# Global keys folded into unused score rows, and q and k of two batches transposed by DMA

## The chip, the cores and the metric

The kernel runs on one core of a Trainium2 chip. The metric is the device time of one execution in microseconds (us), lower is better.

Words used below: PE is the TensorE (PEld its weight loads), DVE the VectorE, ACT the ScalarE, POOL the GpSimd, SP the SyncE, which here only issues DMAs. "L362" is line 362 of that kernel's source; the numbers shift between kernels, so the tile names are the better way to find a group. A DMA transfer is *issued* by an engine and *lands* when the last of its data has arrived. The rows marked PEclk, and the word "clock", give the clock that PE was granted, as a share of full speed.

## The reference, cut to what matters

```python
# B=4, H=8, S=768, D=64, n_global=8, n_local=96
scores = q @ k.T / sqrt(D)
keep   = is_global(key < 8) | is_local(0 <= query - key < 96)
dist   = 96 where global and not local, else |query - key|
a      = softmax(scores - slope[head] * dist, only where keep)
x      = (a @ v) as [B, S, H*D]                    # per batch 768 x 512
theta  = x @ w_theta
y      = w_tok_r @ (x*cos(theta)) + w_tok_i @ (x*sin(theta))
u      = x + y
out    = u + relu(u @ w_ch)
```

A query sees at most 96 keys behind it and the first 8 keys. With tiles of 128 tokens, a tile of 128 keys meets only its own tile of queries and the first 95 queries of the next one.

## The kernel before

The work is a pipeline over batches. While the PE does the second half of batch b (theta, then "mixing" with w_tok, then "chan" with w_ch), it is given the attention of batch b+1 in between. I call the stretch from the first theta product of one batch to the first theta product of the next a *stage*, and name it after the batch whose attention is done in it: the "stage for batch 2" holds the mixing of batch 1 and the attention of batch 2. Three stages follow a start of some 30 us, and the end of batch 3 comes last.

q and k must have their head dimension on the partitions. Before, one load of 768 KB brings each of q and k of a batch, DVE puts a pair of heads in the order that a transpose wants (`qkn`), PE transposes 12 blocks of 128x128, and DVE and ACT copy the result from PSUM:

```python
def prep(b, p, w=0):                        # one pair of heads
    qkn = att.tile([T, NT, 2, 2, D], BF, name="qkn", bufs=3)
    with behind("dve"):
        for i_ in range(2):
            (...)(out=qkn[:, :, i_]..., in_=qk[:, i_, 2 * p:2 * p + 2])
    for i_, dst in ((0, qT), (1, kT)):
        ps = ps_small([T, NT, T], BF)
        with behind("pe"):
            for t_ in range(NT):
                nc.tensor.transpose(ps[:, t_, :], qkn[:, t_, i_]..., ident)
        (vector.tensor_copy for q, scalar.copy for k)(out=dst as (n t), in_=ps)
```

The global keys have scores, exponentials and a value product of their own:

```python
def globals_(b):                            # per batch: 2 bursts of 8 products
    for hh in range(2):
        for p in range(NP):
            nc.tensor.matmul(pg[GS*p:GS*(p+1), c0:c1], lhsT=kT[R, 0:GS], rhs=qT[R, c0:c1])
        nc.scalar.activation(e_, pg[:, 0:S], AF.Exp, bias=gbias...)
        ...
def scores(b, p, c):                        # two tiles of keys, two heads
    ... nc.tensor.matmul(pb[:, hh, j*W:j*W+n], lhsT=kT[R, tile], rhs=qT[R, tile and 96 more])
def values(b, p, hh):                       # per query tile: own, previous, global
    mms = [(e own, vn[it])] + ([(e previous, vn[it-1])] if it else []) + [(eg, vg)]
```

The order in which a stage starts, and the DMA transposes that were there already:

```python
order = rest[:-1] + pre[:2] + th[:2] + pre[2:] + th[2:3] + rest[-1:] + th[3:]
...
nc.sync.dma_start_transpose(out=xT..., in_=x_sb...)   # xtrans, 6 blocks, feeds theta
nc.sync.dma_start_transpose(out=uT, in_=u)            # utrans, 4 blocks, feeds chan
```

q, k and v are loaded by POOL's queue two batches ahead, as soon as their buffers come free. Everything on SP is a DMA issue, done in order: xT, uT, and the output writes.

The softmax here doesn't subtract the row's maximum and nothing guards it: scores larger than these inputs give would overflow.

Of the kernel before, what the change touches and what calls it, by code (L numbers as in the profile page):

```python
# [16 lines left out]
def kernel(  # L17
# [15 lines left out]
    T = 128  # L33
# [26 lines left out]

    loads = {}

    def alloc_loads(b):
        qk = ld.tile([T, 2, H, NT, D], BF, name="qk", bufs=1)
        vn = ld.tile([T, H, NT, D + 1], BF, name="vn")
        nc.vector.memset(vn[:, :, :, D:D + 1], 1.0)
        loads[b] = (qk, vn)

    def load_qk(b, h0, n, which=(0, 1)):
        qk = loads[b][0]  # L70
        for i_ in which:
            nc.gpsimd.dma_start(
                out=qk[:, i_, h0:h0 + n].rearrange("p h t d -> p h (t d)"),
                in_=(q, k)[i_][b, h0:h0 + n].rearrange("h (p t) d -> p h (t d)", p=T))
# [8 lines left out]
    for p in range(NP):  # L83
        load_qk(0, 2 * p, 2)
    load_v(0, 0, 4)
    load_v(0, 4, 4)
# [3 lines left out]
    ones = const.tile([T, W], FP)  # L90
    nc.vector.memset(ones, 1.0)
    ramp = const.tile([T, W], FP)
# [10 lines left out]
    dist = const.tile([T, W], FP)  # L103
    nc.vector.tensor_scalar(dist, ramp, pidx, None, op0=ALU.subtract)
    far = const.tile([T, W], FP)
    nc.vector.tensor_scalar(far, dist, 0.0, None, op0=ALU.is_lt)
    nc.vector.scalar_tensor_tensor(far, in0=dist, scalar=float(NL), in1=far, op0=ALU.is_ge, op1=ALU.add)
    nc.vector.scalar_tensor_tensor(dist, in0=far, scalar=1e6, in1=dist, op0=ALU.mult, op1=ALU.max)
    etab = const.tile([T, H, W], BF)

    def bias_table(p):
        for h in (2 * p, 2 * p + 1):
            nc.scalar.activation(etab[:, h, :], dist, AF.Exp, scale=-slopes[h])


    NE = 4
    e_bufs = [const.tile([T, 2, NT, 2 * T], BF, name=f"e_{i_}") for i_ in range(NE)]
    e_cnt = [0]
    gbias = const.tile([T, 2], FP)
    gmask = const.tile([T, T], BF)  # L120
    shift = const.tile([T, NP, T], BF)
    halfpi = const.tile([T, 1], FP)
    junk = const.tile([T, 1], FP)

    def constants():

        for e_t in e_bufs:
            nc.vector.memset(e_t[:, :, :, W:2 * T], 0.0)


        grel = const.tile([T, T], FP, name="grel")
        nc.vector.tensor_scalar(grel, ramp[:, 0:T], kmod[:, 0:1], None, op0=ALU.subtract)
        for hh in range(2):
            for p in range(NP):
                nc.vector.memset(gbias[GS * p:GS * (p + 1), hh:hh + 1], -float(NL) * slopes[2 * p + hh])

        gneg = const.tile([T, 1], FP, name="gneg")
        nc.vector.tensor_scalar(gneg, grel[:, 0:1], -float(NG), -30000.0, op0=ALU.is_le, op1=ALU.mult)
        nc.vector.tensor_scalar(gbias, gbias, gneg, None, op0=ALU.add)

        gfar = const.tile([T, T], FP, name="gfar")
        nc.vector.tensor_scalar(gfar, grel, float(NL), None, op0=ALU.is_ge)
        nc.vector.scalar_tensor_tensor(gmask, in0=grel, scalar=0.0, in1=gfar, op0=ALU.is_lt, op1=ALU.add)

        nc.vector.memset(shift, 0.0)
        for p in range(NP):
            nc.vector.tensor_copy(out=shift[0:NG, p, GS * p:GS * p + NG], in_=ident[0:NG, 0:NG])
        nc.vector.memset(halfpi, HALF_PI)
# [33 lines left out]
    egs = {}  # L182
# [6 lines left out]

    def prep(b, p, w=0):  # L190
        qk = loads[b][0]
        if (b, 0) not in qkT:
            x_sb[b] = moe.tile([T, NP, NT, T], BF, name="x_sb", bufs=2)
            xT_sb[b] = moe.tile([T, NC, S], BF, name="xT", bufs=1)

        qkn = att.tile([T, NT, 2, 2, D], BF, name="qkn", bufs=3)
# [4 lines left out]
        qT = att.tile([T, S], BF, name="qT", bufs=6)  # L201
        kT = att.tile([T, S], BF, name="kT", bufs=6)
        for i_, dst in ((0, qT), (1, kT)):
            ps = ps_small([T, NT, T], BF)
            with behind("pe"):
                for t_ in range(NT):
                    nc.tensor.transpose(ps[:, t_, :], qkn[:, t_, i_].rearrange("p h d -> p (h d)"), ident)  # L207

            dst = dst.rearrange("p (n t) -> p n t", t=NT)
            src = ps.rearrange("p t n -> p n t")  # L210
            if i_ == 0:
                nc.vector.tensor_copy(out=dst, in_=src)  # L212
            else:
                nc.scalar.copy(out=dst, in_=src)  # L214
            if w:
                warm(w)
        qkT[(b, p)] = (qT, kT)

    def globals_(b):
        eg = []  # L220
        for hh in range(2):
            R = slice(D * hh, D * (hh + 1))
            pg = ps_big().rearrange("p a b -> p (a b)")
            for p in range(NP):
                qT, kT = qkT[(b, p)]
                for c0, c1 in ((0, 512), (512, S)):
                    nc.tensor.matmul(pg[GS * p:GS * (p + 1), c0:c1], lhsT=kT[R, 0:GS],
                                     rhs=qT[R, c0:c1], start=True, stop=True)
            e_ = att.tile([T, S], BF, name=f"eg_{hh}", bufs=2)
            nc.scalar.activation(e_, pg[:, 0:S], AF.Exp, scale=scale, bias=gbias[:, hh:hh + 1])  # L230
            nc.vector.tensor_mul(e_[:, 0:T], e_[:, 0:T], gmask)
            eg.append(e_)
        egs[b] = eg
# [3 lines left out]
    def scores(b, p, c):  # L237
        qT, kT = qkT[(b, p)]
        if c == 0:
            ebuf[(b, p)] = e_bufs[e_cnt[0] % NE]  # L240
            e_cnt[0] += 1
        e_t = ebuf[(b, p)]
        pb = ps_big()
        for j in range(2):
            jt = 2 * c + j
            n = min(W, S - jt * T)
            for hh in range(2):
                R = slice(D * hh, D * (hh + 1))
                nc.tensor.matmul(pb[:, hh, j * W:j * W + n], lhsT=kT[R, jt * T:(jt + 1) * T],  # L249
                                 rhs=qT[R, jt * T:jt * T + n], start=True, stop=True)  # L250
        jt = 2 * c
        if jt + 2 < NT:
            nc.scalar.activation(  # L253
                e_t[:, :, jt:jt + 2, 0:W],
                pb[:, :, 0:2 * W].rearrange("p a (j w) -> p a j w", j=2), AF.Exp, scale=scale)
            nc.vector.tensor_mul(
                e_t[:, :, jt:jt + 2, 0:W], e_t[:, :, jt:jt + 2, 0:W],
                etab[:, 2 * p:2 * p + 2, None, :].to_broadcast([T, 2, 2, W]))
        else:
            nc.scalar.activation(e_t[:, :, jt, 0:W], pb[:, :, 0:W], AF.Exp, scale=scale)  # L260
            last = nc.scalar.activation(e_t[:, :, jt + 1, 0:T], pb[:, :, W:W + T], AF.Exp, scale=scale).ins
            if p == NP - 1:

                with tc.issue_after(last):
                    nc.scalar.activation(junk, halfpi, AF.Sin)
            nc.vector.tensor_mul(e_t[:, :, jt, 0:W], e_t[:, :, jt, 0:W], etab[:, 2 * p:2 * p + 2, :])
            nc.vector.tensor_mul(e_t[:, :, jt + 1, 0:T], e_t[:, :, jt + 1, 0:T],
                                 etab[:, 2 * p:2 * p + 2, 0:T])

    vgs, pos = {}, {}  # L270

    def vglob(b, p):
        vn = loads[b][1]
        pv = ps_small([T, 2, D + 1], FP)
        nc.tensor.matmul(pv, lhsT=shift[:, p, :], rhs=vn[:, 2 * p:2 * p + 2, 0, :],
                         start=True, stop=True)
        vg = att.tile([T, 2, D + 1], BF, name="vg", bufs=4)
        nc.scalar.copy(out=vg, in_=pv)
        vgs[(b, p)] = vg

    def values(b, p, hh):
        vn = loads[b][1]
        e_t = ebuf[(b, p)]
        vg = vgs[(b, p)]
# [6 lines left out]
        for it in range(NT):  # L291
            mms = [(e_t[:, hh, it, 0:T], vn[:, 2 * p + hh, it, :])]
            if it:
                mms.append((e_t[:, hh, it - 1, T:2 * T], vn[:, 2 * p + hh, it - 1, :]))
            mms.append((egs[b][hh][:, it * T:(it + 1) * T], vg[:, hh, :]))
# [94 lines left out]
    def attention_steps(b):  # L390
# [5 lines left out]
        add(1500, globals_, b)  # L396
        for p in range(NP):
            add(150, vglob, b, p)
            if p + 1 < NP:
                add(900, scores, b, p + 1, 0)  # L400
            add(1100, values, b, p, 0)
            if p + 1 < NP:
                add(900, scores, b, p + 1, 1)
            add(1100, values, b, p, 1)
# [25 lines left out]
    with tc.manual_schedule(engines={mybir.EngineType.PE}):  # L430
        warm(8)
        prep(0, 0, 4)
        bias_table(0)
        for p in range(1, NP):
            prep(0, p, 2 if p == 1 else 0)
            bias_table(p)
            if p == 1:
                constants()
            for c in range(NT // 2):
                scores(0, p - 1, c)  # L440
                warm(1)
        globals_(0)
        for p in range(NP):
            vglob(0, p)
        scores(0, NP - 1, 0)
        for p in range(NP):
            values(0, p, 0)
            values(0, p, 1)
            if p < 2:
                scores(0, NP - 1, p + 1)  # L450
            if p:
                xtrans(0, p - 1, nc.scalar.copy)
# [73 lines left out]
```

## Time and profile before

| | before |
|---|---|
| median (lowest to highest) | 193.61 us (193.41 to 193.78) |
| span of the profiled execution | 190.0 us |
| first theta product of batch 0, 1, 2, 3 | 30.5, 77.4, 117.0, 157.2 us |
| stage for batch 1, 2, 3 | 46.9, 39.6, 40.2 us |

The head of the profile page of before: busy time per engine, then the busy tenths of PE and the granted PE clock in 40 slices.

```profile
span 190.0 us, 3965 instructions
PE 174.4 (92%) x1616; PEld 89.8 (47%) x1641; DVE 131.3 (69%) x305; ACT 108.0 (57%) x162; POOL 27.0 (14%) x31
...
PE   7868698999999999999999999999999999999981
PEclk9999999999999999999999999999999999999999
```

PE is at nine tenths from slice 8 on, and its clock is full throughout. The chain of work that ended last, by engine and by line, on the page of before:

```profile
PE 65%; ACT 15%; DVE 8%; DMA 6%; issue 3%; POOL 1%; ACTq 0%; SPq 0%; POOLq 0%
PE ps L352 27%; PE ps L377 10%; PE pb L333 9%; PE pb L298 7%; PE pb L249 5%; DMA uT<-u 3%; PE ps L207 3%; DMA qk<-in_k_dram 3%; ACT cs L337 2%; ACT kT L214 2%; ACT e_108 L253 2%; PE ps L170 2%; DVE qT L212 1%; DVE qkn L199 1%; DVE zri L341 1%
```

Most of the chain is PE work. The busy time by stretch (31 to 76.5, then the stages for batch 2 and batch 3), before. The columns are the stretch, its length, busy us and count of PE, PEld, DVE, ACT and POOL, the PE clock, the DMA share and GB/s:

```profile
31.00:76.50 45.50, 43.74 (x456) 24.74 (x463) 33.97 (x74) 29.07 (x43) 5.79 (x4) 1.00 1.71 156
77.40:117.00 39.60, 38.98 (x364) 19.27 (x368) 29.09 (x62) 24.76 (x36) 1.75 (x2) 1.00 0.92 131
117.00:157.20 40.20, 39.17 (x367) 19.28 (x373) 29.51 (x62) 24.37 (x35) 0.00 (x0) 1.00 0.32 81
```

All that PE waits for in the stage for batch 2, before (engine, line, releaser: us in total, times, longest):

```profile
PE pb L249 <- ACT cs L338: 0.2, 1, 0.2
```

So PE has work all the time, and PE work taken away should shorten a stage, provided that nothing new makes PE wait.

The load of k of batch 3 is issued at 84.02 us and lands at 96.36; the first uT of batch 1 is issued in the middle of it, at 90.87, and lands at 96.87, after 6.0 us in place of the 2.4 us that it takes alone.

### The profile page before, as it was taken

Reading aid. Unit: us, or ns where it says so; the run is one execution under the profiler, and the core shown is the slowest. Engines: PE = TensorE matmul, PEld = TensorE weight load, DVE = VectorE, ACT = ScalarE, POOL = GpSimd, SP = SyncE. Lnnn points to the kernel's source line nnn. Section 1 sums busy time; section 2 is a strip of 40 time slices with the busy share of each in tenths; the row PEclk is TensorE's granted clock in tenths of the full one; section 3 lists DMA queues with packets and bytes.
Section 4 is the critical chain, followed back from the end, with each engine's and each line's share of the span. In section 5 each row is a group of like instructions: output and inputs, shape, how many; then the busy total and the mean of one; then the engine's idle time right before and its main releaser. Section 6 shows DMA issues by size and latency. Waiting matters only on the chain.

```text
span 190.0 us, 3965 instructions
## 1 busy us (share of the span) xinstructions
PE 174.4 (92%) x1616; PEld 89.8 (47%) x1641; DVE 131.3 (69%) x305; ACT 108.0 (57%) x162; POOL 27.0 (14%) x31
## 2 busy tenths in 40 slices
PE   7868698999999999999999999999999999999981
PEld 2434386445735565643354454543554454434430
DVE  4699696487976886996587568986667753734422
ACT  2399987842697764489963450899644704800010
POOL 7992264000030002130000000000000000000000
PEclk9999999999999999999999999999999999999999
DMA  4999999999999833999925458111145254114432
GB/s 61 162 173 158 209 210 208 204 197 146 128 182 219 124 97 100 113 161 192 207 45 120 122 123 131 56 55 31 24 104 124 54 139 141 59 29 109 138 86 110
DMA packets 58082, 23.98 MB, mean 126 GB/s; under 512 B 44240, under 2 KB 54992, under 8 KB 58064
## 3 DMA queue, kind: packets, MB, share of 16 engines
q0 software_dynamic: 35760, 12.85, 72.2%
q1 hardware_dynamic: 22304, 10.88, 23.1%
q8 instruction: 13, 0.21, 0.4%
q14 instruction: 5, 0.04, 0.1%
HBM read 25.69 MB, written 6.29 MB: 168 GB/s over the span
## 4 chain that ended last, share of the span: by engine, by line
PE 65%; ACT 15%; DVE 8%; DMA 6%; issue 3%; POOL 1%; ACTq 0%; SPq 0%; POOLq 0%
PE ps L352 27%; PE ps L377 10%; PE pb L333 9%; PE pb L298 7%; PE pb L249 5%; DMA uT<-u 3%; PE ps L207 3%; DMA qk<-in_k_dram 3%; ACT cs L337 2%; ACT kT L214 2%; ACT e_108 L253 2%; PE ps L170 2%; DVE qT L212 1%; DVE qkn L199 1%; DVE zri L341 1%
## 5 line engine op out<-in xcount | busy, mean ns | idle before, releaser
L352 PE MATMUL ps<-zri,w_tokT_119 128*128 128x512 bf16 x136 | 51.6, 381 | 1.2 <-DVE zri L341 0.5
L352 PE MATMUL ps<-zri,w_tokT_120 128*128 128x512 bf16 x138 | 52.2, 379 | 0.5 <-issue 0.2
L377 PE MATMUL ps<-w_ch_bf,uT 128*128 128x512 bf16 x89 | 23.5, 380 | 1.2 <-DMA uT<-u 0.6
L341 DVE TENSOR_TENSOR zri<-x_sb,cs 128x512 bf16<-128x512 bf16 x48 | 18.3, 422 | 9.1 <-ACT cs L337 7.7
L357 DVE TENSOR_TENSOR u<-x_sb,ps 128x512 bf16<-128x512 bf16 x24 | 16.5, 686 | 11.6 <-PE ps L352 11.1
L333 PE MATMUL pb<-w_theta_bf,xT 128*128 128x512 bf16 x93 | 23.2, 379 | 0.2
L352 PEld LDWEIGHTS <-w_tokT_119 128*128 128x128 bf16 x144 | 14.0, 97 | 17.8 <-issue 4.2
L380 DVE SCALAR_TENSOR_TENSOR o_sb<-ps,u 128x512 f32<-128x512 f32 x24 | 16.5, 686 | 7.5 <-PE ps L377 6.6
L214 ACT COPY kT<-ps 128x768 bf16<-128x768 bf16 x16 | 12.9, 806 | 12.9 <-PE ps L207 12.8
L352 PEld LDWEIGHTS <-w_tokT_120 128*128 128x128 bf16 x144 | 14.1, 98 | 12.5 <-issue 1.4
L371 ACT COPY uT<-ps 128x512 bf16<-128x512 bf16 x7 | 4.1, 587 | 27.0 <-PE ps L370 27.0
L249 PE MATMUL pb<-qT,kT 64*128 64x224 bf16 x192 | 17.2, 254 | 2.3 <-ACT e_110 L253 0.7
L337 ACT ACTIVATE cs<-pb,halfpi 128x1024 bf16<-128x1024 f32 x12 | 13.4, 1119 | 9.1 <-issue 7.2
L207 PE MATMUL ps<-ident,qkn 128*128 128x128 bf16 x192 | 15.0, 222 | 0.9 <-DVE ident L101 0.4
L207 PEld LDWEIGHTS <-qkn 128*128 128x128 bf16 x192 | 11.9, 99 | 7.8 <-DVE qkn L199 5.5
L212 DVE COPY qT<-ps 128x768 bf16<-128x768 bf16 x16 | 15.1, 948 | 0.0
L249 PEld LDWEIGHTS <-kT 64*128 64x128 bf16 x192 | 6.3, 94 | 16.1 <-issue 13.5
L78 POOL DMA_DIRECT2D vn<-in_v_dram x5 | 9.5, 1921 | 24.9 <-DVE rec L306 20.9
L333 PEld LDWEIGHTS <-xT 128*128 128x128 bf16 x96 | 8.9, 98 | 8.8 <-ACT xT L319 0.3
L377 PEld LDWEIGHTS <-uT 128*128 128x128 bf16 x96 | 8.1, 98 | 10.4 <-DMA uT<-u 2.1
L199 DVE COPY qkn<-qk 128x768 bf16<-128x768 bf16 x30 | 10.8, 387 | 3.1 <-DMA qk<-in_q_dram 3.1
L177 PE MATMUL ps<-zero 128*128 128x512 bf16 x28 | 10.4, 473 | 2.4 <-DVE zero L88 1.4
(129 smaller groups left out, 280.9 us busy)
## 6 DMA issues: line engine op xcount, KB each, us to landing
out_dram<-o_sb SPq DMA_DIRECT2D x24, 256.0 KB, 2.3
qk<-in_q_dram POOLq DMA_DIRECT2D x3, 768.0 KB, 8.6
qk<-in_k_dram POOLq DMA_DIRECT2D x3, 768.0 KB, 12.3
vn<-in_v_dram POOLq DMA_DIRECT2D x3, 768.0 KB, 23.5
w_nat<-in_moe_w_tok_r_dram POOLq DMA_DIRECT2D x3, 384.0 KB, 15.9
w_nat<-in_moe_w_tok_i_dram POOLq DMA_DIRECT2D x3, 384.0 KB, 16.8
qk<-in_q_dram POOLq DMA_DIRECT2D x4, 192.0 KB, 5.3
qk<-in_k_dram POOLq DMA_DIRECT2D x4, 192.0 KB, 5.8
```

Of the source, the lines that this page charges most:

```text
L207: nc.tensor.transpose(ps[:, t_, :], qkn[:, t_, i_].rearrange("p h d -> p (h d)"), ident)
L212: nc.vector.tensor_copy(out=dst, in_=src)
L214: nc.scalar.copy(out=dst, in_=src)
L249: nc.tensor.matmul(pb[:, hh, j * W:j * W + n], lhsT=kT[R, jt * T:(jt + 1) * T], rhs=qT[R, jt * T:jt * T + n], start=True, stop=True)
L298: nc.tensor.matmul(o, lhsT=l_, rhs=r_, start=(i_ == 0), stop=(i_ == len(mms) - 1))
L333: nc.tensor.matmul(pb[:, j, :], lhsT=xT[:, dc, st * T:(st + 1) * T], rhs=w_theta_bf[:, dc, :], start=(dc == 0), stop=(dc == NC - 1))
L337: nc.scalar.activation(cs[:, 0], pb, AF.Sin, bias=halfpi)
L341: nc.vector.tensor_mul(zri[b][:, i_, 2 * c + j_, :].rearrange("p (g d) -> p g d", g=NP), xb[:, :, 2 * c + j_, :], cs[:, i_, j_].rearrange( ...
L352: anchor["pe"] = nc.tensor.matmul(ps, lhsT=w_tokT[wi][:, st, tt * T:(tt + 1) * T], rhs=zri[b][:, wi, st, :], start=(st == 0 and wi == 0), ...
L357: anchor["dve"] = nc.vector.tensor_add(u_sb[b, tt].rearrange("p (g d) -> p g d", g=NP), x_sb[b][:, :, tt, :], ps.rearrange("p (g d) -> p g ...
L377: nc.tensor.matmul(ps_c, lhsT=uT[:, dc, :], rhs=w_ch_bf[:, dc, :], start=(dc == 0), stop=(dc == NC - 1))
L380: nc.vector.scalar_tensor_tensor(o_sb, in0=ps_c, scalar=0.0, in1=u, op0=ALU.max, op1=ALU.add)
```

## The change: intent and diff

The intent is to take work from PE, the busiest engine:

1. *Fold.* A tile of 128 keys uses only its last 95 rows for the next tile of queries. Rows 0 to 7 of that product are free, so the 8 global keys are put there (`kG`, a copy of `kT` with the first 8 columns of each tile replaced, and `vG` likewise for the values). The separate scores, exponentials and value products of the global keys go: 17 value products per head become 11.
2. *Batch 2:* the same `qkn` is transposed by one DMA of 12 blocks into `tr`, and DVE and ACT copy `tr` into token order.
3. *Batch 3:* q and k are loaded in token order (16 loads of 96 KB in pieces of 128 bytes), and transposed by two DMAs of 6 blocks a pair, with no copies at all.

```diff
+    way = ["pe", "pe", "dma", "natural"]
...
+        if way[b] == "natural":
+            for h in range(h0, h0 + n):
+                for i_ in which:
+                    nc.gpsimd.dma_start(out=qk[:, i_, h // 2, :, h % 2, :],
+                                        in_=(q, k)[i_][b, h].rearrange("(t p) d -> p t d", p=T))
...
+    def global_keys(kT, kG):
+        nc.vector.tensor_copy(out=kG, in_=kT[:, T:(NT - 1) * T].rearrange("p (t n) -> p t n", t=NT - 2))
+        nc.vector.tensor_copy(out=kG[:, :, 0:NG], in_=kT[:, None, 0:NG].to_broadcast([T, NT - 2, NG]))
...
+        if way[b] == "natural":
+            for i_, dst in ((0, qT), (1, kT)):
+                nc.sync.dma_start_transpose(out=dst..., in_=qk[:, i_, p]...)
+            global_keys(kT, kG)
+            qkT[(b, p)] = (qT, kT, kG)
+            return
-        qkn = att.tile([T, NT, 2, 2, D], BF, name="qkn", bufs=3)
+        qkn = att.tile([T, NT, 2, 2, D], BF, name="qkn", bufs=2)
...
+        if way[b] == "dma":
+            tr = att.tile([T, NT, 2, T], BF, name="tr", bufs=1)
+            nc.sync.dma_start_transpose(out=tr..., in_=qkn...)
         for i_, dst in ((0, qT), (1, kT)):
+            if way[b] == "dma":
+                (nc.scalar.copy if i_ else nc.vector.tensor_copy)(out=dst as (n t), in_=tr[:, :, i_])
+                continue
...
-    def globals_(b):  # removed, with gbias, gmask, shift and constants()
...
             mms = [(e_t[:, hh, it, 0, :], vn[:, h, it, :])]
             if it:
-                mms.append((e_t[..it - 1, T:2 * T], vn[:, 2 * p + hh, it - 1, :]))
-            mms.append((egs[b][hh][:, it * T:(it + 1) * T], vg[:, hh, :]))
+                mms.append((e_t[:, hh, it - 1, 1, :], vG[:, h, it - 2, :] if it > 1 else vn[:, h, 0, :]))
```

At the start the loads, the bias table and the value products of batch 0 are also reordered; the full diff has that too.

## The prediction

> **What bounds it now.** From 31 to 184 us the tensor engine: PE is at 9 tenths in the slices, granted clock 1.0, the chain of waits is 65% PE. Else ACT 15%, DVE 8%.
>
> **What changes, from start-to-start distances of PE instructions in the timeline.**
>
> | per batch | us on PE |
> |---|---|
> | value products, 17 to 11 per head, 31 ns each | -1.5 |
> | global-key scores, two bursts of 0.45 us | -0.9 to -1.1 |
> | shift products of v, 4, with stalls | -0.4 to -0.6 |
> | scores: pairs of heads start 4 ns apart; a pair of 224 columns takes 105 ns; now four pairs of 128, about 57 ns each | +0.3 |
> | transposes of q and k, 8 x 0.37 us (batches 2, 3 only) | -3.0 |
>
> So -2.5 us of PE in the stage that prepares batch 1, -5.7 in those for batches 2 and 3. ACT loses 3 us a batch. DVE gains an estimated 3 us a batch (kG 0.5 us four times, vG about 2, from a 387 ns copy of 768); batch 3 loses 6 us of qkn and qT copies.
>
> **How much is on the path.**
> - Start (0 to 31 us), ACT-bound: global exponentials go, but bias table and exponentials grow. Gain 0.5 us.
> - Stage for batch 1 (31 to 76): DVE, already dense, gets 3 us more. Gain 2 of 2.5.
> - Stage for batch 2 (76 to 117): most of the gain lost. In the built order the transposing DMA queue (SP) holds four 12-block transposes through one buffer, then batch 3's eight 6-block ones, between batch 2's xT and batch 1's uT, and on DVE batch 3's kG copies ahead of batch 1's u. 6 blocks land in 2.75 us, 4 in 2.4, so 12 in about 3.8 (estimate); but with a load in flight uT took 6.0. The Trainium skill ("DMA: Bandwidth & Descriptors", Issuing engines are not separate DMA queues) says that all queues share 16 engines; this agrees. Batch 3's q and k now come in 128-byte pieces: back to back, v in such pieces takes 6.3 us a load, q or k in 768-byte pieces 3.9 (same page, Specifications: line rate needs 512 B). With 16 issues that is some 15 us instead of 8, starting 14 to 17 us into the stage, after the last qkn copy. Batch 3's last transposes then fall 32 to 38 us into a stage that should last 35, and hold up u, uT, xT behind them. Gain 0.5 of 5.7 (-3 to +4).
> - Stage for batch 3 (117 to 157): q and k ready, DVE lighter. Gain 5.
>
> **Prediction: 185.5 us, 8 in 10 between 180.5 and 190.** Faster by over 2%: 0.83; within 2%: 0.16; slower: 0.01.
>
> **What would show it.** Right: 214 matmuls fewer; four score pairs in 0.23 us; theta of batch 0 still starts at 29 to 31 us; the stage for batch 3 5 us shorter; in that for batch 2 PE, DVE or SP wait for transposes (qT, kT, tr, uT). Wrong: no such waits there and that stage over 4 us shorter (then 180 or less).
>
> **What would make it wrong.** The 128-byte load landing early (near 180); transposes and load slowing each other more than assumed (near 190); DVE binding in the stage for batch 1; odd 65-element rows slowing vG copies.

## More of the kernel before

In the trace of before, the load of v of batch 3 is issued at 74.66 us and lands at 85.56 us.

An output write issued at 77.66, beside the load of v, took 5.55 us, and one with little beside it (105.34) took 2.29.

## The result, and the profile after

| | before | after |
|---|---|---|
| median (lowest to highest), same chip | 193.51 us (193.34 to 193.78) | 207.98 us (206.08 to 208.53) |
| ratio, 95% interval | | 1.073 (1.066 to 1.080): slower |
| first theta product of batch 0, 1, 2, 3 | 30.5, 77.4, 117.0, 157.2 | 29.6, 76.4, 138.7, 173.3 us |
| stage for batch 1, 2, 3 | 46.9, 39.6, 40.2 | 46.8, 62.3, 34.6 us |

A ratio is always the mean time of one kernel's fast runs over the mean of the other's fast runs of the same rounds, so it is not quite the ratio of the medians quoted. The changed kernel was run a second time as a control, in later rounds: 208.40 us, ratio 1.076 (1.071 to 1.081), with PE waits of 7.0 and 5.1 us in the stage for batch 2, as expected. Its stage for batch 2 took 61.9 us, with the half clock (below) for 20.4 us of it. What was expected of it:

> The changed kernel once more, as the control of the next run on the same chip: ratio 1.073 to 1.08, PE waiting about 7 us at 83 us for zri and 5 to 6 us at 125 us, the clock at half for 15 us or more of 83 to 140 us.

The start is 0.9 us shorter, the stage for batch 1 is unchanged, the stage for batch 3 is 5.6 us shorter, and the stage for batch 2 is 22.7 us longer. The head of the page after:

```profile
span 206.5 us, 3533 instructions
PE 166.3 (81%) x1405; PEld 85.1 (41%) x1427; DVE 134.4 (65%) x297; ACT 103.6 (50%) x118; POOL 39.3 (19%) x45
...
PE   6855868899999999129668782699999999999982
PEclk9999799999999999957979999579999999999998
```

PE has less to do, and a hole: the slices from 16 to 25. The clock row shows a second cost, whose size was not measured: during or after a wait, PE is granted only half its clock for a while. In the stage for batch 2 those stretches add up to 17.0 us (6.8, 3.4 and 6.8). The chain after:

```profile
PE 41%; DMA 23%; DVE 18%; POOL 7%; ACT 6%; issue 2%; SPq 1%; ACTq 0%; POOLq 0%
PE ps L362 19%; PE ps L387 8%; DMA tr<-qkn 7%; DMA qk<-in_k_dram 6%; DMA kT<-qk 6%; PE pb L343 5%; POOL qk L79 4%; PE pb L308 4%; PE pb L260 3%; DVE e L272 3%; DVE qT L235 3%; POOL qk L83 2%; DVE x_sb L318 2%; ACT cs L347 2%; DMA out_dram<-o_sb 2%
```

DMA rose from 6% to 23%. Busy time by stretch, after, with the columns as above:

```profile
31.00:76.50 45.50, 42.78 (x439) 24.63 (x448) 37.03 (x83) 28.01 (x34) 6.48 (x4) 1.00 1.77 152
76.40:138.70 62.30, 40.27 (x295) 18.52 (x298) 33.84 (x73) 26.87 (x26) 14.15 (x16) 0.86 1.28 142
138.70:173.30 34.60, 33.94 (x291) 16.52 (x296) 24.99 (x47) 19.86 (x21) 0.00 (x0) 1.00 0.35 88
```

In the middle line PE has 295 products in place of 364, but 22 us of it are waits and the clock is 0.86. In the last line everything works as intended. The longest PE waits in the stage for batch 2, after:

```profile
PE ps L362 <- DVE zri L351: 8.7, 3, 7.2
PE pb L308 <- DVE x_sb L318: 5.6, 1, 5.6
PE pb L308 <- ACT e L264: 2.5, 1, 2.5
PE ps L387 <- DMA uT<-u: 2.0, 2, 1.2
```

None of these names a transpose of q or k. One has to ask further what DVE and ACT waited for. The same stretch, waits of DVE and ACT, after:

```profile
ACT kT L223 <- DMA tr<-qkn: 11.1, 3, 8.7
DVE qT L223 <- DMA tr<-qkn: 10.3, 4, 7.9
DVE kG L193 <- DMA kT<-qk: 9.2, 4, 3.4
```

The first wait closely, in the timelines after, PE and then DVE (start, length, engine, line, operation, idle time before it and releaser):

```profile
82.86 0.38 PE L362 MATMUL ps<-zri,w_tokT_110 128*128 128x512 bf16 x1
90.44 0.58 PE L362 MATMUL ps<-zri,w_tokT_111 128*128 128x512 bf16 x1 [7.20 <-DVE zri L351]
```

```profile
80.74 0.42 DVE L351 TENSOR_TENSOR zri<-x_sb,cs 128x512 bf16<-128x512 bf16 x1
89.07 0.98 DVE L223 COPY qT<-tr 128x768 bf16<-128x768 bf16 x1 [7.91 <-DMA tr<-qkn]
89.95 0.44 DVE L351 TENSOR_TENSOR zri<-x_sb,cs 128x512 bf16<-128x512 bf16 x1
```

DVE stands at `qT<-tr` for 7.9 us, with a `zri` behind it that PE needs. The chain of waits after, from 77 us, shows what came last (start, length, what):

```profile
77.47 11.58 DMA tr<-qkn
89.05 0.02 issue
89.07 0.98 DVE qT L223
90.05 0.34 DVE zri L351
...
104.65 3.96 DMA qk<-in_k_dram
108.61 7.58 DMA kT<-qk
```

A 12-block transpose takes 3.76 us when little is in flight (the second one: 90.78 to 94.53). The first took 11.58, beside the load of v of batch 3, issued at 73.32 and landed at 89.56.

### The profile page after: what moved, and what is told of

It is laid out like the page before. It is cut to its first block, busy times and chain, and to the rows that moved or that the text cites. A ratio compares the mean times of both kernels' runs of the same rounds, so it can differ in the third digit from the quotient of the medians.

```text
span 206.5 us, 3533 instructions
## 1 busy us (share of the span) xinstructions
PE 166.3 (81%) x1405; PEld 85.1 (41%) x1427; DVE 134.4 (65%) x297; ACT 103.6 (50%) x118; POOL 39.3 (19%) x45
## 4 chain that ended last, share of the span: by engine, by line
PE 41%; DMA 23%; DVE 18%; POOL 7%; ACT 6%; issue 2%; SPq 1%; ACTq 0%; POOLq 0%
PE ps L362 19%; PE ps L387 8%; DMA tr<-qkn 7%; DMA qk<-in_k_dram 6%; DMA kT<-qk 6%; PE pb L343 5%; POOL qk L79 4%; PE pb L308 4%; PE pb L260 3%; DVE e L272 3%; DVE qT L235 3%; POOL qk L83 2%; DVE x_sb L318 2%; ACT cs L347 2%; DMA out_dram<-o_sb 2%
## 5 line engine op out<-in xcount | busy, mean ns | idle before, releaser
L362 PE MATMUL ps<-zri,w_tokT_111 128*128 128x512 bf16 x141 | 54.5, 389 | 8.3 <-DVE zri L351 7.4
L264 ACT ACTIVATE e<-pb 128x1024 bf16<-128x1024 f32 (+1 forms) x48 | 44.2, 958 | 23.4 <-PE pb L260 23.4
L362 PE MATMUL ps<-zri,w_tokT_110 128*128 128x512 bf16 x131 | 50.9, 393 | 2.6 <-DVE zri L351 2.0
L387 PE MATMUL ps<-w_ch_bf,uT 128*128 128x512 bf16 x93 | 25.7, 394 | 2.4 <-DMA uT<-u 2.2
L362 PEld LDWEIGHTS <-w_tokT_110 128*128 128x128 bf16 x144 | 14.4, 100 | 23.5 <-issue 10.2
L260 PE MATMUL pb<-qT,kT 64*128 64x128 bf16 x224 | 17.4, 227 | 6.9 <-ACT e L264 5.0
L308 PEld LDWEIGHTS <-e 128*128 128x128 bf16 x352 | 15.1, 102 | 16.5 <-DVE x_sb L318 6.3
L272 DVE TENSOR_TENSOR e<-e,etab 128x1024 bf16<-128x1024 bf16 (+1 forms) x32 | 19.6, 614 | 1.4 <-ACT e L264 1.4
L308 PE MATMUL pb<-vn,e 128*128 128x65 bf16 x168 | 13.2, 201 | 9.0 <-DVE x_sb L318 5.6
L260 PEld LDWEIGHTS <-kT 64*128 64x128 bf16 x224 | 9.8, 96 | 21.8 <-issue 17.8
L260 PE MATMUL pb<-qT,kG 64*128 64x128 bf16 x128 | 13.2, 225 | 2.4 <-DVE kG L194 2.4
L348 ACT ACTIVATE cs<-pb 128x1024 bf16<-128x1024 f32 x12 | 12.3, 1024 | 0.0
```

The source lines that it names most:

```text
L260: nc.tensor.matmul(pb[:, hh, o:o + T], lhsT=lhsT, rhs=qT[R, (own, nxt)[part]], start=True, stop=True)
L264: ins = nc.scalar.activation(e_c, pb[:, :, 0:n], AF.Exp, scale=scale).ins
L272: nc.vector.tensor_mul(e_c, e_c, tab[:, :, s0:s0 + n // T].rearrange("p a s n -> p a (s n)"))
L308: nc.tensor.matmul(o, lhsT=l_, rhs=r_, start=(i_ == 0), stop=(i_ == len(mms) - 1))
L348: nc.scalar.activation(cs[:, 1], pb, AF.Sin)
L362: anchor["pe"] = nc.tensor.matmul(ps, lhsT=w_tokT[wi][:, st, tt * T:(tt + 1) * T], rhs=zri[b][:, wi, st, :], start=(st == 0 and wi == 0), ...
```

## The experiments

All kernels gave correct results, and each was timed in three rounds beside the kernel before. The kernels ran on several chips, on which the kernel before took 193 to 195 us, so the ratios compare better across runs than the times. Edits are against the changed kernel unless said otherwise. "Stage for batch 2" is read from the profile of each. The us are the median of all executions; in e2, e4, e10, e12 and e13 one of these was slow, and the ratios leave it out.

| run | batch 2 | batch 3 | v of batch 3 | us | ratio | stage for batch 2 |
|---|---|---|---|---|---|---|
| before | PE | PE | | 193.5 | 1 | 39.6 |
| e1_fold | PE | PE | | 191.64 | 0.985 | 41.9 |
| e2_dma2 | DMA | PE | | 203.31 | 1.042 | (profile slow) |
| e3_nat3 | PE | token order, DMA | | 195.91 | 1.005 | 50.8 |
| after | DMA | token order, DMA | | 207.98 | 1.073 | 62.3 |
| e4_vearly | DMA | token order, DMA | early | 202.72 | 1.041 | 54.4 |
| e12_tr_unused | DMA, unread; PE | PE | | 205.56 | 1.059 | 55.3 |
| e13_tr_late | DMA, copies later | PE | | 206.01 | 1.059 | 56.4 |
| e15_dma2_natpe | DMA | token order, PE | | 200.92 | 1.034 | 52.2 |
| e16_dma2_natpe_vearly | DMA | token order, PE | early | 196.07 | 1.011 | 47.8 |
| e9_natload_pe | PE | token order, PE | | 188.09 | 0.976 | 39.0 |
| e14_nat23_pe | token order, PE | token order, PE | | 186.10 | 0.963 | 37.8 |

### The parts alone: e1_fold, e2_dma2, e3_nat3

```diff
-    way = ["pe", "pe", "dma", "natural"]
+    way = ["pe", "pe", "pe", "pe"]         # e1_fold
+    way = ["pe", "pe", "dma", "pe"]        # e2_dma2
+    way = ["pe", "pe", "pe", "natural"]    # e3_nat3
```

> The fold alone: q and k of all four batches go through PE transposes as before; the global keys stay folded into the score rows and the start keeps its new load order. Theory A (the loss is the DMA transposes: they collide with loads in flight, and in-order queues behind them make PE wait) expects about 188 us (187 to 191): equal to before up to 76 us, then 2.7 us of PE work saved in each of the next two stages. Theory B (the fold is the loss, DVE having 3 us more a batch) expects 193 us or more.

> Batch 2 by DMA as in the changed kernel, batch 3 by PE as before. Theory A: the stall of 7 us before the mixing of batch 1 stays (the 12-block transpose lands after 11 to 12 us beside the load of v of batch 3), the later stalls at 100 to 131 us mostly go: about 198 us (195 to 201). Theory B: as the fold alone, 193 or more, with little on top. If only batch 3's load and transposes matter: about as the fold alone.

> Batch 2 by PE, batch 3 loaded in token order and transposed by DMA. The load of batch 3 can start when batch 2's qkn copies are done, some 8 us into the stage instead of 20, and the SP queue has no 12-block transposes ahead. Theory A: few stalls remain, and PE saves 3 us more than with the fold alone: 187 us (184 to 191). Rival (the 128-byte load and its eight transposes are the loss by themselves, whatever stands before): 195 us or more.

Measured: 191.64 us (0.985, 0.980 to 0.989), 203.31 (1.042, 1.036 to 1.048) and 195.91 (1.005, 0.998 to 1.011). The fold alone gains 1.5% here. By the ratios, batch 2 by DMA costs 5.7 points more than that (some 11 us; a point is 1% of the time of before) and batch 3 by DMA 2.0 points (some 4 us). Added to the fold they make 1.062; the change measured 1.073 in its own rounds, so the two together cost the sum or up to a point more.

In e3 the stage for batch 3 has the intended length (34.7 us), and the loss is one wait in the stage for batch 2 (PE waits of e3):

```profile
PE ps L387 <- DMA uT<-u: 10.9, 2, 10.7
```

Here `uT` of batch 1 stood on the SP queue behind transposes of batch 3's q and k, and then took 9.2 us from issue to landing.

### Is it the load of v: e4_vearly

```diff
-        vn = ld.tile([T, H, NT, D + 1], BF, name="vn")
+        vn = ld.tile([T, H, NT, D + 1], BF, name="vn", bufs=3)
-            vGs[b] = att.tile([T, H, NT - 2, D + 1], BF, name="vG", bufs=2)
+            vGs[b] = att.tile([T, H, NT - 2, D + 1], BF, name="vG", bufs=1)
```

> The changed kernel with a third buffer for v (and one vG buffer to pay for it), so that v of batch 3 lands before about 65 us and is not in flight beside the first 12-block transpose; the orders on PE, ACT, SP and DVE are otherwise the same. Theory A: that transpose lands in about 4 us instead of 11.6, 6 to 7 us of PE idle time go, and some of the throttled clock with it: 199 us (197 to 202). Rival (12 blocks through one buffer are slow by themselves): it still takes over 8 us and the time stays at 205 to 208.

Measured: 202.72 us (1.041, 1.032 to 1.050). With a third buffer for v, its load is done before the stage for batch 2 begins. The PE wait of 7.2 us becomes two of 1.0 and 1.5, and the stage 54.4 us in place of 62.3. The load of v in front of the first transpose is thus a real part of the loss, about a third of it by the length of the stage. The later waits stay (3.4 us at 95, 5.0 at 118.8).

### Does the start matter: e5_fold_order, e6_fold_vearly

e5 is the fold alone with the load order of before at the start; e6 is e5 with the two buffer edits of e4.

```diff
-    load_qk(0, 0, 2); load_qk(0, 2, 2); load_v(0, 0, 4)
-    load_qk(0, 4, 2); load_qk(0, 6, 2); load_v(0, 4, 4)
+    for p in range(NP):
+        load_qk(0, 2 * p, 2)
+    load_v(0, 0, 4); load_v(0, 4, 4)
```

> The fold alone with the start's load order of before (all q and k ahead of v). In the fold alone PE idles 2.45 us at 12.3 us, waiting for the q and k of heads 4 to 7, which now stand behind half of v (k of heads 6, 7 landed at 16.9 us, before at 13.2 us), and mixing of batch 0 starts at 37.2 us, before at 35.7. If that order is the loss at the start: mixing starts about 1.5 us earlier and the time is 1.5 us under the fold alone, ratio about 0.977. Rival (the start is bound by DVE and ACT work that the fold adds): as the fold alone, ratio 0.985, or slower since v comes later for the value products that now stand early.

> The run before, with a third buffer for v (one vG buffer): v of batch 3 lands before 65 us, so q and k of batch 3 land some 5 us earlier (about 92 us) and the first uT of batch 1, which took 8.55 us beside them in the fold alone and held PE 2.84 us, takes at most 4. Theory A: 2 to 3.5 us under the run before (no PE wait over 1 us at 96 us, clock never at half there). Rival (that wait is not from loads in flight): no change.

Measured: 192.42 us (1.000, 0.995 to 1.005) and 193.39 us (1.002, 0.997 to 1.006). Both theories miss. The start did not get shorter in e5: PE waits 3.0 us for the first `kG` instead of 2.4, and the clock is half for 10.2 us after it. In e6 the wait for `uT` at 97 us stays (3.0 us, and 2.7 in e5); the load of q and k, not that of v, is in flight there (85.54 to 100.11 us). With e1 these runs say that the fold alone is worth between nothing and 1.5%; the chip and the load order of the start differ between them, so which of the two makes the difference is not shown.

### Can the wait be moved away: e7_nat3_uTpe, e10_nat3_late

Both start from e3. e7 transposes u of batch 1 on PE, so that no DMA stands between u and chan. e10 places the transposes of batch 3 behind the last uT of batch 1 on SP, and the kG copies behind the last u of batch 1 on DVE.

```diff
-            if b and (b, tt) != (B - 1, NT - 1):       # e7, in utrans
+            if b > 1 and (b, tt) != (B - 1, NT - 1):
```

```diff
-                nc.sync.dma_start_transpose(out=dst..., in_=qk...)   # e10, in prep
-            global_keys(kT, kG)
+            with behind("sp"):                   # anchor: the newest uT transpose
+                ... the two transposes
+            with behind("dve"):                  # anchor: the newest u
+                global_keys(kT, kG)
```

> Batch 3 in token order by DMA transposes (as in the run e3_nat3), but u of batch 1 transposed on PE, so that no matmul of that stage waits on the SP queue. In e3_nat3 PE idled 10.67 us at 95.7 us for uT, which stood behind two pairs of qT and kT and landed after 9.2 us. If the order on SP is what reaches PE: that wait goes, PE work grows by 1.3 us, and DVE's waits for kT (4.1 and 7.0 us in e3_nat3, in front of x_sb and e) become the next bound: 190 us, ratio 0.975 (0.965 to 0.99). Rival (DVE's waits for kT alone cost as much): ratio 1.00 as e3_nat3.

> Batch 3 in token order by DMA transposes (as e3_nat3), but its eight transposes queued on SP behind the last uT of batch 1 and its kG copies on DVE behind the last u of batch 1: by then the load has landed, and nothing of batch 1 or 2 stands behind them. If order alone made these transposes costly, PE's waits of over 2 us in the stage of batch 1 go and the gain of the fold and of 3 us less PE work remains: ratio 0.965 (0.955 to 0.975), 1 point under e9_natload_pe (0.976). Rival (eight transposes and a token-order load cost by themselves): ratio 0.99 or above.

Measured: e7 200.43 us (1.039, 1.033 to 1.044), worse than e3. The wait is as long and has another name (PE waits of e7):

```profile
PE ps L380 <- DVE u L367: 11.4, 3, 10.4
```

Before that `u`, DVE stands at `kG` copies that wait for transposes of k (4.8 and 6.0 us). So there were two routes of about the same length, and closing one is not enough. (Why e7 is slower than e3 was not followed up; over the stages for batches 2 and 3 together its PE is busy for 75.2 us and not 73.0.) e10 closes both at once by order alone: 190.35 us (0.984, 0.980 to 0.989), between the two expectations.

### Is it only the clock: e8_warm

```diff
+            if b == 1 and tt == 0:
+                main.append((0, lambda: warm(32)))     # idle products before the mixing of batch 1
```

> The changed kernel with 32 matmuls on zeros (6.9 us at full clock) on PE just ahead of the mixing of batch 1, where PE otherwise stands still for 7.2 us: the wait is the same, only PE's idling is filled. If the half clock after that wait costs time of its own, the clock stays at 1.0 from 83 to 95 us and the time falls by 1 to 3 us against the changed kernel on the same chip; if the clock is only a mark of the waiting, the time is the same or up to 1 us longer.

Measured: 210.67 us (1.087, 1.080 to 1.093). No gain, and if anything 2 us worse than the control on the same chip. The 32 products fill 83.8 to 90.9 us, the clock stays full until 100 us, but then PE waits 7.4 us for exponentials, because ACT stands at `kT<-tr`, and half clock follows for 17 us. The test does not separate the price of the half clock from that of the waits; it shows that holding the clock over the first wait brings nothing while the later ones remain. The control is a hint: it had the half clock 3.4 us longer than the first profile of the same kernel (20.4 and 17.0 us), and its stage was 0.4 us shorter.

### The load without the DMA transposes: e9_natload_pe, e11_natload_pe_vg

Batches 0 to 2 on PE; batch 3 is loaded in token order, and PE transposes straight from the loaded tile. e11 adds a change of DVE order at the start (vG behind the first table product).

```diff
-    way = ["pe", "pe", "dma", "natural"]
+    way = ["pe", "pe", "pe", "natural"]
...
-                nc.sync.dma_start_transpose(out=dst..., in_=qk[:, i_, p]...)
+                ps = ps_small([T, NT, T], BF)
+                with behind("pe"):
+                    for t_ in range(NT):
+                        nc.tensor.transpose(ps[:, t_, :], qk[:, i_, p, t_]..., ident)
+                (nc.scalar.copy if i_ else nc.vector.tensor_copy)(out=dst..., in_=ps)
```

> Batch 3 loaded in token order, in the same 128-byte pieces, but transposed on PE from the loaded tile: load and transposes taken apart. Theory A (the transposes, and what stands behind them on SP, are the loss; the load only stretches what is in flight beside it): uT of batch 1 is issued at about 90 us and not 97, lands by 99, PE waits about 3 us there as in the fold alone: ratio 0.985 (0.975 to 0.992). Rival (the 128-byte load by itself): ratio 1.00 or above.

> The run e9_natload_pe with the first vG copy of batch 0 queued on DVE behind the first score product. There it stood ahead of the first kG copy and waited 4.56 us for v, PE waited 4.01 us for that kG, and ACT's first score exponential started at 15.4 us (before: 12.6). Same mechanism at the start of the kernel: the wait goes, mixing of batch 0 starts 2 to 3 us earlier than in e9_natload_pe (39.1 us), ratio 0.963 (0.955 to 0.97). Rival (the start is bound by the amount of ACT and DVE work): ratio 0.976 as there.

Measured: 188.09 us (0.976, 0.970 to 0.982) and 189.28 us (0.977, 0.971 to 0.983). Loading in token order did no harm and probably helps: it makes the `qkn` copies needless, and `uT` of batch 1 lands after 4.6 us beside it. The intervals of e9 and e1 touch; that of e14 below, with two batches loaded so, lies clear of e1. The transposes by DMA were the bad half: e3 and e9 differ in nothing else, and stand at 1.005 and 0.976. e11 misses: the first `kG` wait falls from 4.0 to 1.8 us, but PE then waits 1.4 us for vG, and half clock lasts 17.1 us at the start instead of 10.2.

### Is it the waiting copies: e12_tr_unused, e13_tr_late

My theory so far was that the copies `qT<-tr` and `kT<-tr` cost time because they wait in front of other work. Both runs have batch 3 on the old path, so they compare with e2 (ratio 1.042).

```diff
         for i_, dst in ((0, qT), (1, kT)):             # e12: tr is written, nobody reads it
-            if way[b] == "dma":
-                (...)(out=dst..., in_=tr[:, :, i_]...)
-                continue
```

```diff
+        if way[b] == "dma":                            # e13: prep ends after the transpose
+            fetch[(b, p)] = tr, qT, kT, kG
+            qkT[(b, p)] = (qT, kT, kG)
+            return
...
+    def take(b, p):       # the copies and kG: pair 0 behind the last cos, sin and zri,
+        ...               # later pairs behind exps and table products of the pair before
-            order = rest[:-1] + pre[:2] + th[:2] + pre[2:] + th[2:3] + rest[-1:] + th[3:]
+            order = rest[:-1] + pre[:2] + th[:3] + rest[-1:] + th[3:] + pre[2:]
         # and tr bufs=3, vG bufs=1; qkn of pairs 2 and 3 behind a table product
```

> Global keys folded everywhere, q and k of batch 3 on the path of before, and for batch 2 the four transposes by DMA are issued just as in the change, but nobody reads what they write: q and k of batch 2 are transposed on the TensorE from the same tile. So the DMA traffic and the place on the SP queue are kept, and the waiting for the landing is gone. Theory (what costs is that copies stand waiting for the landing in front of other work on VectorE and ScalarE): 191 to 194 us, that is near the fold alone (191.6), no PE wait over 3 us in 80 to 117. Rival (the transfers themselves, or the SP queue blocked by them, delay the loads, uT and xT): 198 us or more, near the 203 of batch 2 by DMA.

> As batch 2 by DMA alone (203.3 us), but the copies that put the transposed q and k in token order are moved: those of pair 0 behind the last cos, sin and zri of batch 1, those of the later pairs behind the exps and table products of the pair before, with three buffers for the transposed tile (one buffer of vG less to make room). Each still waits for its landing, but little independent work stands behind it. Theory (order on VectorE and ScalarE): the wait of 7 us at the first mixing product of batch 1 goes, and 193 to 197 us. Rival (the transposes land too late for the scores whatever stands where): 199 us or more, with the TensorE waiting for exp or for qT at the scores of batch 2 instead.

Measured: 205.56 us (1.059, 1.051 to 1.067) and 206.01 us (1.059, 1.050 to 1.067). The theory falls, as far as these two runs go: each took a wait away and brought another. The PE waits of e12, and below of e13, in the stage for batch 2:

```profile
PE ps L225 <- DVE qkn L215: 7.7, 1, 7.7
PE ps L382 <- DMA uT<-u: 6.5, 1, 6.5
```

```profile
PE ps L400 <- DMA uT<-u: 9.2, 2, 7.8
PE pb L271 <- DVE qT L250: 4.8, 1, 4.8
```

In e12 the third `qkn` copy cannot begin until the first transpose has read the buffer, and DVE waits 7.8 us for that. Then `uT` waits. So the late transpose hands its delay on through whatever touches it: its readers, its source buffer, or the next transfer. And the second wait is now the same in both: `uT`.

The landings of e12 and e13 show what was in flight. Times are us from the start:

| run | transfer | issued | landed | the load beside it: issued, landed |
|---|---|---|---|---|
| e12 | uT of batch 1 | 102.64 | 111.34 | k of batch 3: 94.67, 109.95 |
| e13 | uT of batch 1 | 95.26 | 106.70 | k of batch 3: 92.55, 106.49 |
| e1 | uT of batch 1 | 90.16 | 98.72 | k of batch 3: 84.94, 98.45 |
| after | tr of batch 2, pair 0 | 77.47 | 89.05 | v of batch 3: 73.32, 89.56 |

In these four cases a transfer that takes 2.4 or 3.8 us alone lands within 1.4 us of the load beside it. That looks like a transfer that waits until the load has landed. The packets of the DMA queues, which the traces hold too, show something else: the two take turns. In e13, first with transposes alone (91.5 to 93 us) and then with transposes beside the load of q and k (95 to 105 us), by queue: packets, MB, share of the DMA engines. q1 is the queue of SP, q0 that of POOL:

```profile
q1 hardware_dynamic: 1226, 0.31, 109.6%
...
q0 software_dynamic: 1895, 1.44, 92.7%
q1 hardware_dynamic: 1788, 0.45, 34.6%
```

Beside the load the transposes move 179 packets a microsecond in place of 817, nearly as many as the load (190). In e12 and e13 `uT` also stands behind 12-block transposes on SP's own queue.

In the trace after, the first 12-block transpose is 1536 packets of 256 bytes. They run from 81.86 to 87.95 us, so they begin 4.4 us after the issue and take 6.1 us. Those of the second, alone, begin 1.2 us after the issue and take 2.0 us. The load is slowed as well: v of batch 3 takes 15.6 to 16.3 us in the runs with a 12-block transpose beside it (after, its control, e8, e12, e13, e15) and 10.9 to 13.1 us without (before, e1, e3, e5, e7, e9, e17). Nor does the order of issue decide: before, an xT issued at 75.25 us, 0.6 us after the load of v, landed at 78.02, well ahead of it (85.56). Part of the late beginning is the queue of SP itself, where an output write stands ahead of the transpose; why that write began late (its first packet at 80.6 us, issued at 77.04) is not shown.

In e12 the sum fits too, as an estimate: from 93.8 us on, q and k (3.9 us each, from landings back to back before, at 36.08, 39.96 and 43.82 us) and two 12-block transposes (3.76 us each) make 15.3 us, that is 109.1; the last of them landed at 110.3.

### Is it the backlog of loads: e15_dma2_natpe, e16_dma2_natpe_vearly, e17_fold_paced

e15 is e9 with batch 2 transposed by DMA as in the change. e16 is e15 with the two buffer edits of e4. e17 is the fold alone with the load of q and k of batch 3 in eight parts.

```diff
-    way = ["pe", "pe", "pe", "natural"]     # from e9
+    way = ["pe", "pe", "dma", "natural"]    # e15; e16 adds vn bufs=3, vG bufs=1
```

```diff
-        load_qk(b, 0, 8)                    # e17, from e1
+        for p in range(NP if b == 3 else 0):
+            load_qk(b, 2 * p, 2)
+        if b < 3:
+            load_qk(b, 0, 8)
```

> The change as it is for batch 2 (transposes by DMA), while batch 3 is loaded in token order in sixteen small loads and transposed on the TensorE: no transposes by DMA of batch 3 and no large load of q and k behind which uT could stand. Theory (a transfer lands only when what was issued before it has landed; so the waits come from transposes that stand behind a large load): the wait at the first mixing product of batch 1 stays at 6 to 8 us, because the first transpose still stands behind the load of v; the later waits go; 196 to 200 us. Rival (the transposes of batch 2 are too slow and serial in themselves, whatever load is beside them): waits of more than 5 us in all between 90 and 125, and 201 us or more.

> As the run before, and v of batch 3 also lands early (three buffers of v, one of vG), so that the transposes by DMA of batch 2 stand behind no large load at all. Theory (the backlog ahead of the transposes is the whole cost): no PE wait over 2 us after 40, and 188 to 193 us. Rival (the transposes cost beyond the backlog: serial over one buffer, ScalarE copies of 1.7 us in place of 0.8): 195 us or more.

> The fold alone (191.6 us), with the load of q and k of batch 3 cut into eight parts of two heads each, same bytes, same pieces, no transposes by DMA of q and k at all. Theory (backlog): the parts are issued about 0.8 us apart, so less stands ahead of uT of batch 1, which lands within 5 to 7 us instead of 8.6; the PE wait of 2.8 us at 96 falls below 1.2, and 189 to 191 us. Rival (the size of one issue does not matter, only the bytes in flight): wait 2.3 us or more, and 191 to 193 us.

Measured: 200.92 us (1.034, 1.028 to 1.039), 196.07 us (1.011, 1.003 to 1.019) and 191.13 us (0.982, 0.976 to 0.988).

e15: between the two. The wait at the first mixing product stays, 6.5 us, as the theory says, and no PE wait after it is longer than 2.9 us, in place of 5.6. But the waits between 90 and 125 us still add up to some 7 us, more than the 5 that the rival asked for, and the time lies just above the range of the theory and just below that of the rival.

e16: the rival holds. With no large load beside the first of them, the transposes of batch 2 still cost 8.0 us against e9 (196.07 and 188.09, on two chips; by the ratios 3.5 points, or 6.8 us). PE waits no longer than 2.6 us at a time, the clock is half for 10.2 us in the stage, and the chain runs through the transposes. Its landing times and copies:

```profile
L223 SPq DMA_TRANSPOSE tr<-qkn x4: 1280/1455/1606, 78.1 to 97.3; - x4
L227 ACT COPY kT<-tr x4: 1648/1680/1702, 83.4 to 104.4; 128x768 bf16<-128x768 bf16 x4
...
DMA to landing us min/median/max: 3.7/5.1/7.1
```

From the first transpose issued (78.1) to the last landed (104.4) it takes 26 us for four pairs, one after another through one buffer: issue, 3.7 to 7.1 us to land, a copy of 1.7 us on ACT, then the next. On PE the same four pairs were done by 84 us (the copies `kT<-ps` before start from 78.6 to 83.4). The last two pairs are not free of traffic: they land after 5.0 and 7.1 us, beside the sixteen small loads of batch 3 (issued from 90.65 us on), so this run does not show what the transposes cost with nothing in flight. How the 8 us divide between the serial chain, that traffic and the slower ACT copy was not tried.

e17: the rival holds again. `uT` of the fold alone, with the load in eight parts:

```profile
  PE ps L387: 2.8, 1
...
DMA to landing us min/median/max: 2.4/3.8/8.6
```

The parts are issued from 83.66 to 88.63 us and the last lands at 98.11; `uT`, issued at 89.75, lands at 98.31. The wait of 2.8 us is untouched. Cutting a load into parts does not help when the parts are issued faster than they drain (here the first took 3.4 us to land and the last 9.5); what is in flight beside the transfer stays the same. In e9 sixteen parts of half the size come one every 0.8 us, and `uT` lands after 4.6 us.

### A version that beats both: e14_nat23_pe

e9 with batch 2 loaded in token order as well.

```diff
-    way = ["pe", "pe", "pe", "natural"]
+    way = ["pe", "pe", "natural", "natural"]
```

> Token-order loads with transposes on the TensorE for batch 2 as well as batch 3, no transposes by DMA of q and k at all. Theory (the gain of the token-order load, 191.6 to 188.1 us for one batch, is VectorE work taken away and a load that lets the small transfers through, so a second batch gains again): 184.5 to 187.5 us. Rival (in the stage for batch 2 the TensorE has no wait that VectorE makes, and the sixteen loads come in the prologue, where they delay w_ch, xT and v): 188 to 191 us.

Measured: 186.10 us (185.25 to 187.33), 0.963 (0.956 to 0.969): faster than before by 3.7% and than the change by over a tenth. Its stages for batch 2 and 3, columns as above:

```profile
76.80:114.60 37.80, 36.83 (x342) 19.32 (x346) 29.49 (x59) 22.78 (x26) 13.37 (x16) 1.00 1.37 146
114.60:151.00 36.40, 35.09 (x317) 17.81 (x321) 27.39 (x56) 22.24 (x25) 0.00 (x0) 1.00 0.41 80
```

PE has no wait worth naming in either, and the clock stays full from 18.5 to 182.3 us.

## Why the prediction was wrong, point by point

- **Start, "Gain 0.5".** Right: 0.9 us (first theta product at 29.6 against 30.5).
- **Stage for batch 1, "Gain 2 of 2.5".** Wrong: 0.1 us (46.8 against 46.9). PE is busy 1.0 us less in 31 to 76.5 us, and DVE 3.1 us more, as the prediction said it would be; the first mixing product comes 1.4 us later (37.1 against 35.7). That DVE took the gain was named as a risk and is likely, but no run tests it.
- **Stage for batch 2, "Gain 0.5 of 5.7 (-3 to +4)".** This is the step that failed, by size. Its input was the landing time of a transpose, 3.8 us, where the first one beside a load took 11.58, and its result was a stage in which PE then stood still for 22 us. The mechanism was named: transposes that share the DMA engines with loads, the SP queue, kG copies ahead of u. The term measured a *loss of 22.7 us* (62.3 against 39.6). Three parts of it, each from a pair of runs, in points of the ratio (one point is 1.9 us). The second and the third pair differ by one edit, the first by two; each difference is uncertain by about a point, and only the second pair is known to have run on one chip:

| part | pair | points | us |
|---|---|---|---|
| transposes of batch 2 by DMA, no large load beside the first | e9 to e16 (which also has v early) | 3.5 | 6.8 |
| the load of v beside the first of them | e16 to e15 | 2.2 | 4.3 |
| transposes of batch 3 by DMA instead of on PE | e15 to after | 3.9 | 7.6 |

  They add up to 9.7 points, 18.7 us, between e9 and the change. What e9 keeps is the fold and the load in token order. The parts are not independent: with batch 3 transposed by DMA, the load of v is worth 3.2 points (e4 to after) and not 2.2.
- **"so 12 in about 3.8 (estimate)".** Right for a transpose with little beside it: 3.76 us. The mistake was to use it where a load was in flight. The prediction wrote down that uT took 6.0 us "with a load in flight", but put no such factor on the 3.8. In the trace of before, the load of v was in flight until 85.56 us, the first transpose was going to be issued at about 77.5, and two transfers beside a load took some 2.4 to 2.5 times as long as alone (6.00 against 2.4, 5.55 against 2.29). That makes some 9 us (estimate), still short of the 11.58 measured, but enough to see DVE and ACT stand still with zri behind them.
- **"Batch 3's last transposes then fall 32 to 38 us into a stage that should last 35".** The time of 126.6 us for the last issue is 50 us into the stage. It came later since POOL's loads of batch 3 began at 96 us, after qkn copies that had waited themselves: one late transfer delays the next.
- **Stage for batch 3, "Gain 5".** Right: 5.6 us (34.6 against 40.2); PE is busy 5.2 us less there, 5.7 forecast.
- **"What would show it".** The signs named for "right" came: 211 matmuls fewer in the trace (214 forecast), theta of batch 0 at 29.6 us, the stage for batch 3 shorter by 5.6 us, and waits for transposes in that for batch 2. They tell whether the mechanism acts, not how much it costs, so they could not warn of this loss.
- **The clock** was not in the prediction. In the stage for batch 2 it is half for 17.0 us. How much of the loss this is was not separated; e8_warm tried and did not.
- **Chances.** "Slower" was given 0.01. The range -3 to +4 for the one uncertain stage was far too narrow for a stage in which a dozen new transfers stood between engines that wait in order.

What stays open: the share of the half clock in the loss, the division of the 6.8 us of batch 2's own transposes, why a transfer beside a load begins so late, and why order alone (e10_nat3_late) brings back most but not all of batch 3's loss.

## What to carry to other kernels

Moving work from the busiest engine to DMA is not free when the result has to come back within the same stage: a small transfer beside a large load shares the DMA engines with it packet by packet, whatever queue the load came from, and here one of 3.8 us took 11.6. So look in the trace for the loads in flight at the moment when the new transfer will be issued, and for what other transfers took beside them. A late transfer stops more than its reader, because engines work in order and because it holds its source buffer; removing one of its waits (e7, e12, e13) only moved the delay to the next. When several transfers land together, count their packets before concluding that one waits for the other. Split a change into its parts before judging it: here the fold and the load in token order cost nothing or gained, and only the transposes by DMA were bad.

## What the Trainium skill lacked or had wrong

- "DMA: Bandwidth & Descriptors", section "Issuing engines are not separate DMA queues", says that DMAs of all engines run on the same 16 DMA engines and interleave. The trace agrees; the section gives no figure for what it costs. In e17 a transpose that takes 2.4 us alone took 8.6 beside a load (issued 89.75, landed 98.31, the load 98.11).
- The same page, "Queues, rings and completion order", says that an engine takes turns between queue rows packet by packet. The traces agree: in 10 us of e13 the SP queue moved 1788 packets and the POOL queue 1895. What the page lacks is the cost for a transfer of many small packets, and a word on a late beginning: the 12-block transpose took 11.58 us beside a load and 3.76 alone, and its first packet came 4.4 us after the issue instead of 1.2.
- The same page, "Latency and other measured facts", gives a bandwidth for DMA transposes (261 GB/s in one kernel), and no time for small ones. Here 4 blocks of 128x128 in bf16 took 2.42 us, 6 took 2.75 and 12 took 3.76, with little else in flight: about 1.7 us fixed and 0.17 us a block (32 KB), as an estimate some 195 GB/s beyond the fixed part.
- "SBUF — State Buffer", section "Door 1: The DMA port swizzle", says that strided access to SBUF pays for each new line of 16 bytes. ACT copying 128x768 from the transposed tile in SBUF took 1.69 us, and the copy of the same shape and order from PSUM 0.80 us (before), which would fit; but DVE took 0.98 against 0.95 us for the same. I found no page that gives the cost of such a read, or says that it is dear for ACT and not for DVE; no run here tests the cause.
- "TensorE: Matmul & The Clock Gate", section "What's actually happening", gives windows of about 3.4 us for the clock gate. The runs agree: half-clock stretches of 3.4, 6.8, 10.2 and 17.1 us, all multiples of 3.4. The page speaks of a whole idle window; in the fold alone a PE wait of 2.8 us at 95.9 us was followed by a stretch of 3.4 us at half clock.
